# An attention and MLP-mixer block on one core: a unit's first P V products are held back one block where the copy of the preceding unit's sums is far off

## The chip, the cores and the metric

The kernel runs on one core of one Trainium2 chip. The metric is the device time of the whole kernel in microseconds (us); it is one launch.

## What is computed

The reference normalizes `x` (2048 rows of 512 values), scales and shifts it with values made from `c`, and adds attention with 32 heads of 16 values; then it normalizes again and adds a mixer and an MLP. The part that matters here is the attention:

```
q, k, v = qkv[0], qkv[1], qkv[2]                      # 32 heads, 2048 rows, 16 values
scores = einsum("bhqd,bhkd->bhqk", q, k) * (Dh ** -0.5)
p = softmax(scores, axis=-1)
o = einsum("bhqk,bhkd->bhqd", p, v)
x = x + ga * (o.reshape(B, S, D) @ wo)
h = layernorm(x) * (1 + cb) + sb
x = x + gb * mixer_and_mlp(h, w1, w2, w3, w4)
```

## The kernel before

**Stages.** The first 139 us make the first parts of Q, K and V. Attention runs from 139 to 1531 us; its first quarter still has Q, K, V and weight work mixed in as filler, its last 80 us the first rows of the tail. From 1531 us on come the output projection, the mixer and the MLP.

**Units and steps.** Attention has 64 units: four groups of 512 queries times 16 pairs of heads. A unit has 16 key tiles of 128 keys, one step `s` for each, and each step has two halves `j`, one for each head of the pair. For a half, TensorE makes the scores (`sc`, L1009: 128 keys by 512 queries), and beside it, in other rows of the array, the scores of a half 24 steps later in the other orientation (`mb`, L993), of which only the row maximum is wanted. VectorE reduces each `mb` to maxima (`mx`, L989). ScalarE makes the exponential of each `sc` as a 32-bit whole number (`pt`, L1005). The upper and the lower 16 bits of `pt` are used as two f16 operands. The lower ones need a conversion, once for each step over both halves: on GpSimd (L1058), or on ScalarE (the planner's helper, L153) when the planner thinks GpSimd is more than 200 ns further behind than ScalarE (`p_low`).

**P V.** TensorE multiplies `pt` with V into one accumulator `pv` in PSUM. A part with the upper bits of one step is four small matmuls side by side (L1083, called V below); a part with the lower bits of two steps is four more (L1080, called L). A unit has 16 V and 8 L, in the order V V L. There is one accumulator bank for all units: after a unit's last L, ScalarE copies it out (`ac`, L1100, in `ac_copy`), and only then the next unit's first V may write it. Later TensorE sums the copy's rows (`ot`, L1110, eight matmuls in the trace), ScalarE copies that (`sm`, L1117), VectorE takes reciprocals (`rc`, L1125) and GpSimd scales (`osb`, L1121).

**Buffers.** Seven PSUM banks serve `sc` and `mb` in turn (`NSM = 7`; `ot` takes one too), the eighth is the accumulator. There are six `pt` buffers, so the exponential of step s writes where step s-6 was, and has to wait for that step's V and L.

**The order.** The program is written out by hand-made planning in Python at build time: a planner (`Sched`) keeps an estimated time for TensorE (`T["P"]`), ScalarE, VectorE and GpSimd, with fixed costs in ns, and each engine then executes its queue strictly in the order written. Attention is written in blocks. A block is first the *rows*, three halves with their six matmuls (`sc` and `mb`), and then the *column*, all P V parts that are at least two blocks old, one to three of them. A unit has 32 halves and a block 3, so the pattern of blocks against units repeats every 32 blocks, which are three units. At the top of a block stands the accumulator's copy if a unit ended in the block ahead of it; it joins ScalarE's queue ahead of the block's own exponentials. `v_free` is the planner's time at which that copy is done. In the kernel before, the column's loop (L1615) takes parts in order, and stops only ahead of a unit's first V if other parts are already in the same column.

Of the kernel before, what the change touches and what calls it, by code (L numbers as in the profile page):

```python
# [21 lines left out]
P = 128  # L22
KT = D // P
NKT = S // P
# [47 lines left out]
LNPC = 1  # L72
W0G = 1
WSPL = 1
NLOW = 1
CLOW = 1150
OUTW = 7000.0
# [250 lines left out]
def kernel(ctx, tc, A_x, A_wqkv, A_wo, B_w1, B_w2, B_w3, B_w4, c, w_mod, out):  # L328
# [58 lines left out]
    for j in range(2):  # L387
        x = [ident[:, 64 * j + VD * a:64 * j + VD * a + DH + 1] for a in range(3)]
# [29 lines left out]
    sch = Sched()  # L418
# [74 lines left out]
    def load_wm(j):  # L493
# [6 lines left out]
        w = w_mod[:, j * D:(j + 1) * D].rearrange("(k p) n -> p k n", p=P)  # L500
        n = KT // (WSPL if j < 2 else 1)
        for k in range(0, KT, n):
# [395 lines left out]
    def drain(flag):  # L898
        while flag not in done:
            sch.step()  # L900
# [70 lines left out]
    e_exp, e_hi, e_low, v_free, acs = {}, {}, {}, [0.0], []  # L971
# [39 lines left out]
    def row_pair(s, j):  # L1011

        parts = []
        if 0 <= s < NS:
            parts.append((j, score_part(s, j)))
        if s + LEAD < NS:
            parts.append((1 - j, max_part(s + LEAD, 1 - j)))
        parts = [x for _, x in sorted(parts, key=lambda x: x[0])]

        def mms():  # L1020
            for _, mm, _ in parts:
                mm()
        e = sch.put("P", CROW, max(x[0] for x in parts), mms)
        return [partial(x[2], e) for x in parts]
# [20 lines left out]
    def p_low(s):  # L1045

        p = pt[s].rearrange("p j n -> p (j n)")
        o, i = p.bitcast(F16)[:, 0::2], p.bitcast(U16)[:, 0::2]
        ready = e_exp.pop(s) + XX
        g, a = [max(sch.T[e], ready) for e in "GA"]  # L1050
        if g > a + LACT:

            for h in range(NLOW):
                n = 2 * CH // NLOW
                c = slice(h * n, (h + 1) * n)
                e_low[s] = XP["A"] + sch.crit("A", CLOW, ready, partial(act.activation, o[:, c], i[:, c], AF.Copy, scale=0.5))
        else:
            e_low[s] = XP["G"] + sch.crit("G", 1345, ready, lambda: pool.tensor_scalar(  # L1058
                o, i, 0.5, 1.0, op0=OP.mult, op1=OP.mult))

    def pv_ready(s, lo):

        return max(e_low[s], e_low[s + 1]) if lo else max(e_hi.pop(s), v_free[0] if s % NKT == 0 else 0.0)

    def pv_part(s, lo):


        u, kt = divmod(s, NKT)
        if kt == 0 and not lo:
            pv[u] = ap_.tile([P, CH], F32, name="pv", tag="v", bufs=1)  # L1070
        v, acc = vst[u], pv[u]

        def mms():
            for j in range(2):
                for i in range(2):
                    r = 64 * j + 32 * i
                    if lo:
                        c = 128 + 32 * j + (0 if i else 8)
                        n = min(32, 192 - c)
                        te.matmul(acc[r:r + n, :], v[:, kt + i, c:c + n].bitcast(F16), pt[s + i].bitcast(F16)[:, j, 0::2],  # L1080
                                  start=False, stop=kt == NKT - 2, skip_group_check=True)
                    else:
                        te.matmul(acc[r:r + 32, :], v[:, kt, r:r + 32], pt[s].bitcast(F16)[:, j, 1::2],  # L1083
                                  start=kt == 0, stop=False, skip_group_check=True)
        e = sch.put("P", CCOL, 0.0, mms)
        if lo:
            for i in range(2):
                pt.pop(s + i)
                e_low.pop(s + i)
            if kt == NKT - 2:  # L1090
                acs.append((u, e + COUT))

    def ac_copy():
        u, e = acs.pop()
        while u and ("ot", u - 1) not in done:
            sch.step()
        ac = at.tile([P, CH], F32, name="ac", tag="ac", bufs=1)
        vst.pop(u)
        acc = pv.pop(u)
        e = sch.crit("A", cA(), e + PX, lambda: act.activation(ac, acc, AF.Copy))  # L1100
        v_free[0] = e + XP["A"]
        sch.add(o_fin(u, ac, e + XP["A"]), 0)
# [168 lines left out]
    def tail_loads():  # L1271
        rings["0"] = Ring(FRONT, [], "r")
        for _ in range(BR):
            rings["0"].add([("wr", BR)])
            yield sch.wait(T0W)
        for t in range(TPC):
            x1t[t] = fa.tile([P, D], F32, name="x1", tag="x1", bufs=X1F)
            act.dma_start(x1t[t], x_d[t * P:(t + 1) * P])
# [298 lines left out]
    def before(s):  # L1577

        nu, r = divmod(s + 32, 16)
        if r == 0 and 0 < nu < NU:  # L1580
            ci, pr = units[nu]
            drain(("kq", pr // 4))
            if ci:
                drain(("q", pr // 8))
            load_unit(nu)
        nu, r = divmod(s + 6, 16)
        if r == 0 and 0 <= nu < NU:
            drain(("v", units[nu][1] // 8))
            load_v(nu)
        if s == -12:  # L1590
            unit_tiles(at, 2, dve, pool)
# [4 lines left out]
    pvs = [x for s in range(0, NS, 2) for x in ((s, 0), (s + 1, 0), (s, 1))]  # L1596
    due = 0.0
    for k, blk in enumerate(blocks + [[]] * (LAG + CPER)):
        if blk and blk[0] <= LENDS <= blk[-1]:
            sch.most = MOST  # L1600
        for x in blk:
            if x % 2 == 0:
                if x == blk[0]:
                    before(x // 2)
                if x >= 0 and x % 32 == 0:
                    drain(("shift", x // 32))
        if acs:
            ac_copy()
        row = [divmod(x, 2) for x in blk if x < 2 * NS]
        s0 = row[0][0] if row else 0  # L1610
        col = []
        if k >= LAG and (k % CPER == 0 or not blk):

            x = (blocks[min(k - LAG, len(blocks) - 1)] or [-1])[-1]
            while pvs and 2 * (pvs[0][0] + pvs[0][1]) < x and not (col and pvs[0][0] % NKT == 0 and not pvs[0][1]):  # L1615
                col.append(pvs.pop(0))
        t, start = CIN, 0.0
        need = sum((s >= 0) + (s + LEAD < NS) for s, _ in row)
        sch.flush(need)
        banks = sorted(sm.t)  # L1620
        n = 0
        for s, i in row:
            n += (s >= 0) + (s + LEAD < NS)

            start = max(start, banks[n - 1 + 2 * (s < 0)] - t)
            t += CROW
        t += CMID
        for s, i in col:
            start = max(start, pv_ready(s, i) - t)
            t += CCOL  # L1630
        sch.gap(start)
        sch.flush(need)
        sch.T["P"] = max(sch.T["P"], start) + CIN
        low = sorted(e_exp)
        for s, i in row:
            for fn in row_pair(s, i):
                fn()
        for x in blk[1:]:
            if x % 2 == 0:
                before(x // 2)  # L1640
        for s in low:
            p_low(s)
        sch.T["P"] += CMID
        for s, i in col:
            pv_part(s, i)
        sch.T["P"] += COUT
        for e in "ADG":
            sch.misc(e, max(sch.T["P"], sch.T[e]) + TOLE[e])
        if s0 < 0:
            sch.fill(LEADB / 2 * len(blk))  # L1650
        elif sch.gens:
            late = s0 >= NS - T0S
            due += RATE3 if late else RATE if s0 < NS // NC else RATE2
            if due >= (BURST3 if late else BURST if s0 < NS // NC else BURST2):
                sch.fill(due)
                due = 0.0
        if 2 * (NS // NC) - 1 in blk:
            for key in (("v", 1), ("kq", 3), ("q", 0), ("q", 1), "pieces"):
                drain(key)
            qpx.close()  # L1660
            sch.gapmin = GAPMIN2
            ot = o0x.enter_context(tc.tile_pool(name="ot", bufs=1, side="right"))
            for ci in range(1, NC):
                oh[ci] = ot
                osb[ci] = ot.tile([P, TPC, D], F32, name=f"osb{ci}", tag=f"osb{ci}", bufs=1)
            fa = o0x.enter_context(tc.tile_pool(name="fa", bufs=1, side="right"))
            big = {"A4": fa.tile([P, 4 * KT * 2 * P], F32R, name="A")}
            big["A"] = big["A4"]
        if blk and blk[0] <= 2 * (NS - T0L) <= blk[-1]:
            sch.add(tail_loads())  # L1670
        if blk and blk[0] <= 2 * (NS - T0S) <= blk[-1]:
            sch.add(tail(0))
# [54 lines left out]
```

## Time and profile before

| | us |
|---|---|
| median of 3 runs | 2030.32 (2027.38 to 2033.31) |
| the profiled execution | 2025.04 |
| its span, first to last instruction | 2023.3 |
| busy: TensorE, VectorE, GpSimd, ScalarE | 1936.2, 1658.3, 1568.8, 1511.5 |
| granted TensorE clock, mean | 0.990 |

The profiled execution is 5.3 us below the median and has 1.7 us outside its span. In the profile's rows PE is TensorE, PEld its weight loads, DVE VectorE, ACT ScalarE, POOL GpSimd. A row of the timeline has the start, the length, the engine, the line and operation, how many instructions were merged, and in brackets the idle time ahead of the first and what ended it. The matmuls of a merged row overlap each other, so a busy TensorE is not one at its peak.

### The profile page before, as it was taken

How to read it: one execution, taken by the hardware profiler on the slowest of the kernel's cores; microseconds unless marked ns; L12 is line 12 of the kernel's file. 1: busy time of each engine (PE TensorE's matmuls, PEld its weight loads, DVE VectorE, ACT ScalarE, POOL GpSimd, SP SyncE). 2: the span in 40 equal slices, each digit the busy share in tenths (PEclk: the TensorE clock that was granted, in tenths of full speed). 3: DMA queues.
4: the chain of work that ended last, by engine and by line, in shares of the span. 5: the costliest groups of instructions: out<-in, count | busy, mean ns of one | idle time of the engine just before them, and what ended most of it. 6: DMA issues, size and time to landing. Idle time of an engine off the chain costs nothing. (4 is left out here: it accounts for less than half of the span.)

```text
span 2023.3 us, 41663 instructions
## 1 busy us (share of the span) xinstructions
PE 1936.2 (96%) x14456; PEld 1166.2 (58%) x14456; DVE 1658.3 (82%) x2979; ACT 1511.5 (75%) x3085; POOL 1568.8 (78%) x1488
## 2 busy tenths in 40 slices
PE   8999999999999999999999999999998889999999
PEld 5755545454444444444444444444447778888998
DVE  6398788879999999999999999999965786656443
ACT  6438887768999999999999999989984554434443
POOL 6349988879999999999999999999994554425222
PEclk9989999999999999999999999999999999999999
DMA  8877666545353435353434343454414676653541
GB/s 303 234 202 184 156 187 165 133 129 124 72 107 72 107 72 107 72 107 72 101 78 92 87 93 86 93 157 100 90 38 146 233 271 262 233 184 124 189 165 68
DMA packets 185508, 278.01 MB, mean 137 GB/s; under 512 B 117104, under 2 KB 127856, under 8 KB 169008
## 3 DMA queue, kind: packets, MB, share of 16 engines
q1 hardware_dynamic: 181792, 267.20, 49.0%
q10 hardware_dynamic: 2304, 4.20, 0.6%
q0 software_dynamic: 1200, 3.93, 0.5%
q8 instruction: 115, 1.88, 0.4%
q14 instruction: 97, 0.79, 0.1%
HBM read 211.81 MB, written 62.91 MB: 136 GB/s over the span
## 5 line engine op out<-in xcount | busy, mean ns | idle before, releaser
L989 DVE TENSOR_REDUCE mx<-mb 128x1 f32<-128x512 f32 x2048 | 1250.2, 684 | 71.8 <-PE mb L993 62.7
L1058 POOL TENSOR_SCALAR pt<-pt 128x1024 f16<-128x1024 uint16 x953 | 1247.9, 1366 | 77.9 <-ACT pt L1005 74.7
L1005 ACT ACTIVATE pt<-sc 128x512 int32<-128x512 f32 x2048 | 1061.1, 615 | 122.8 <-PE mb L993 97.2
L993 PE MATMUL mb<-kst,qtl 62*128 62x512 f32 x2048 | 780.9, 461 | 21.4 <-ACT pt L1005 9.9
L1009 PE MATMUL sc<-qtl,kst 64*128 64x512 f32 x2048 | 738.7, 448 | 4.2 <-DVE mx L989 1.8
L993 PEld LDWEIGHTS mb<-kst,qtl 62*128 62x128 f32 x2048 | 359.1, 193 | 234.0 <-ACT pt L1005 160.2
L1009 PEld LDWEIGHTS sc<-qtl,kst 64*128 64x128 f32 x2048 | 335.9, 185 | 184.0 <-DVE mx L989 115.5
L1083 PE MATMUL pv<-pt,vst 128*32 128x512 f16 x4096 | 384.6, 397 | 20.6 <-ACT ac L1100 20.6
L1456 POOL TENSOR_TENSOR g<-sq,g 128x256 fp32r<-128x256 f32 (+1 forms) x124 | 98.0, 794 | 184.5 <-ACT g L1455 174.7
L1080 PE MATMUL pv<-pt,vst 128*32 128x512 f16 (+1 forms) x2048 | 221.0, 389 | 2.5 <-POOL pt L1058 2.4
L1083 PEld LDWEIGHTS <-vst 128*32 128x32 bf16 x4096 | 91.7, 93 | 226.6 <-issue 208.1
L358 PE MATMUL w<-A,wr 128*128 128x256 f32 (+1 forms) x520 | 155.6, 300 | 0.1
L356 PE MATMUL w<-A,wr 128*128 128x256 f32 (+1 forms) x520 | 155.4, 300 | 0.2 <-ACT A L350 0.2
L360 PE MATMUL w<-A,wr 128*128 128x256 f32 (+1 forms) x520 | 155.0, 299 | 0.0
L1452 ACT ACTIVATE sq<-w 128x256 f32<-128x256 f32 (+1 forms) x130 | 52.1, 402 | 123.2 <-PE w L360 113.9
L356 PE MATMUL w<-wr,g 128*128 128x512 f32 x270 | 106.7, 395 | 2.4 <-DMA wr<-Ws 2.4
L360 PE MATMUL w<-wr,g 128*128 128x512 f32 x270 | 106.2, 393 | 0.2 <-POOL g L1456 0.2
L358 PE MATMUL w<-wr,g 128*128 128x512 f32 x270 | 106.2, 393 | 0.0
L1434 DVE SCALAR_TENSOR_TENSOR sq<-sq,w 128x256 f32<-128x256 f32 (+1 forms) x130 | 58.1, 449 | 54.2 <-ACT sq L1454 53.8
L356 PEld LDWEIGHTS w<-A,wr 128*128 128x128 f32 x520 | 100.8, 194 | 1.5 <-ACT A L350 0.5
L358 PEld LDWEIGHTS w<-A,wr 128*128 128x128 f32 x520 | 100.9, 194 | 1.2 <-DVE A L346 0.4
L360 PEld LDWEIGHTS w<-A,wr 128*128 128x128 f32 x520 | 100.8, 194 | 0.5 <-issue 0.5
(156 smaller groups left out, 2124.9 us busy)
## 6 DMA issues: line engine op xcount, KB each, us to landing
wr<-Ws SPq DMA_DIRECT2D x66, 1024.0 KB, 5.9
vst<-Vs SPq DMA_DIRECT2D x64, 768.0 KB, 5.7
kst<-Ks SPq DMA_DIRECT2D x126, 384.0 KB, 6.3
Ws<-wr SPq DMA_DIRECT2D x14, 1024.0 KB, 6.3
qtl<-Qs SPq DMA_DIRECT2D x128, 96.0 KB, 4.4
Vs<-vt SPq DMA_DIRECT2D x32, 384.0 KB, 4.4
Ks<-qk SPq DMA_DIRECT2D x16, 512.0 KB, 4.0
Qs<-qk SPq DMA_DIRECT2D x16, 512.0 KB, 3.0
```

Source lines behind the costliest of these rows:

```text
L356: te.matmul(o, lh, rh, start=first, stop=False)
L358: te.matmul(o, lh, rl, start=False, stop=False)
L360: te.matmul(o, ll, rh, start=False, stop=last)
L989: end = sch.crit("D", 605, e + PX, lambda: dve.reduce_max(mxs[u][:, j, g, c:c + 1], b, axis=AX.X))
L993: return ready, lambda: te.matmul(b, lhs, kst[u % 3][r, c * CH:(c + 1) * CH], start=True, stop=True), after
L1005: ea = sch.crit("A", 480, e + PX, lambda: act.activation(pt[s][:, j], b, AF.Exp))
L1009: return ready, lambda: te.matmul(b, kst[u % 3][r, kt * P:(kt + 1) * P], qst[u][r], start=True, stop=True), after
L1058: e_low[s] = XP["G"] + sch.crit("G", 1345, ready, lambda: pool.tensor_scalar(o, i, 0.5, 1.0, op0=OP.mult, op1=OP.mult))
L1080: te.matmul(acc[r:r + n, :], v[:, kt + i, c:c + n].bitcast(F16), pt[s + i].bitcast(F16)[:, j, 0::2], start=False, stop=kt == NKT - 2, skip ...
L1083: te.matmul(acc[r:r + 32, :], v[:, kt, r:r + 32], pt[s].bitcast(F16)[:, j, 1::2], start=kt == 0, stop=False, skip_group_check=True)
L1434: dve.scalar_tensor_tensor(sq, sq, 1.0, b, op0=OP.add, op1=OP.mult)
L1456: ("G", cG(n), lambda: pool.tensor_tensor(lo, sq, hi, op=OP.subtract)), (None, 0, end), bank=b)
```

## The change

A constant `VLATE = 1500.0` is added. Ahead of a unit's first V the column now also stops where it is still empty, if the block has rows and the planner expects the accumulator's copy to be done more than 1500 ns after TensorE's present time:

```diff
+VLATE = 1500.0
...
-            while pvs and 2 * (pvs[0][0] + pvs[0][1]) < x and not (col and pvs[0][0] % NKT == 0 and not pvs[0][1]):
+            while pvs and 2 * (pvs[0][0] + pvs[0][1]) < x:
+                if pvs[0][0] % NKT == 0 and not pvs[0][1] and (col or row and v_free[0] > sch.T["P"] + VLATE):
+                    break
                 col.append(pvs.pop(0))
```

The parts come in a fixed order, so such a block has rows alone, and the next block's column has the parts of both. This happens at 20 of the 63 unit starts, counted from 0: units 1, 4, 5, 7 and 15, and then every third from 19 to 61. Since the planner's times differ from there on, other instructions move too. In the rows below line numbers of the changed kernel are one higher than before (L1084 is V, L1081 is L, L994 `mb`, L1010 `sc`, L1101 the copy, L1111 `ot`, L154 the conversion on ScalarE).

**TensorE, end of unit 54, the block in which the copy is late.** Before:

```order
L993 MATMUL mb<-kst_1105,qtl_1103 128x512
L1009 MATMUL sc<-qtl_965,kst_967 128x512 x2
L993 MATMUL mb<-kst_1105,qtl_1103 128x512 x2
L1009 MATMUL sc<-qtl_965,kst_967 128x512
L1083 LDWEIGHTS vst
L1083 MATMUL pv<-pt,vst 32x512
```

and in the changed kernel:

```order
L994 MATMUL mb<-kst_1105,qtl_1103 128x512
L1010 MATMUL sc<-qtl_965,kst_967 128x512 x2
L994 MATMUL mb<-kst_1105,qtl_1103 128x512 x2
L1010 MATMUL sc<-qtl_965,kst_967 128x512 x2
L994 MATMUL mb<-kst_1105,qtl_1103 128x512 x2
L1010 MATMUL sc<-qtl_965,kst_967 128x512 x2
L994 MATMUL mb<-kst_1105,qtl_1103 128x512
L1084 LDWEIGHTS vst
L1084 MATMUL pv<-pt,vst 32x512
```

Before, six score matmuls are followed by V V L, six more, and V. Now twelve score matmuls stand together, and V V L V behind them.

**TensorE, where the copy of unit 54 is summed (`ot`).** Before:

```order
L1083 MATMUL pv<-pt,vst 32x512
L1110 MATMUL ot<-smat,ac 128x34 x4
L993 MATMUL mb<-kst_1105,qtl_1103 128x512
L1009 MATMUL sc<-qtl_965,kst_967 128x512 x2
L993 MATMUL mb<-kst_1105,qtl_1103 128x512 x2
L1009 MATMUL sc<-qtl_965,kst_967 128x512
```

and now:

```order
L1084 MATMUL pv<-pt,vst 32x512
L1111 MATMUL ot<-smat,ac 128x34 x4
L1010 MATMUL sc<-qtl_965,kst_967 128x512
L994 MATMUL mb<-kst_1105,qtl_1103 128x512 x2
L1010 MATMUL sc<-qtl_965,kst_967 128x512 x2
L994 MATMUL mb<-kst_1105,qtl_1103 128x512
```

`ot` stood ahead of the rows of the second block after the late copy (they begin with `mb`); now it stands one block later (rows that begin with `sc`).

**ScalarE, end of unit 15, where nothing is held back.** Before:

```order
L1005 ACTIVATE pt<-sc 128x512 x21
L153 ACTIVATE pt<-pt 128x1024
L1100 ACTIVATE ac<-pv 128x512
L1005 ACTIVATE pt<-sc 128x512 x6
L1117 ACTIVATE sm<-ot 128x136
```

and now:

```order
L154 ACTIVATE pt<-pt 128x1024
L1006 ACTIVATE pt<-sc 128x512 x12
L1101 ACTIVATE ac<-pv 128x512
L1006 ACTIVATE pt<-sc 128x512 x6
L1118 ACTIVATE sm<-ot 128x136
```

The conversion stood right ahead of the copy; now twelve exponentials lie between them. The copy of unit 12 has lost its conversion in the same way. In all, ScalarE has 76 conversions instead of 71 and GpSimd 948 instead of 953; every other kind of instruction has the same count as before.

## The prediction

> **What bounds the kernel now.** I read the busy time by stage first. The columns are PE, PEld, DVE, ACT and POOL busy us (with counts), then the granted clock and the DMA share:
>
> ```profile
> 139.30:480.00 340.70, 331.84 (x2575) 178.10 (x2575) 284.69 (x485) 272.72 (x565) 304.91 (x261) 1.00 0.62 162
> 480.00:1458.00 978.00, 947.14 (x8064) 448.96 (x8064) 938.55 (x1632) 904.22 (x1792) 938.25 (x801) 1.00 0.44 93
> 1531.00:2023.30 492.30, 463.54 (x2715) 415.67 (x2713) 298.34 (x595) 213.60 (x489) 199.34 (x287) 0.98 0.51 188
> ```
>
> The change acts in the first two rows. In the long one, 978 us, three engines are equally full: TensorE 96.8%, VectorE and GpSimd 96.0%. None has much idle time to give, and VectorE's 39 us (978 - 938.55) and GpSimd's 40 us bound what any reordering there can bring. In the first row TensorE alone is full (97.4%). Next the list of waits, of the whole run:
>
> ```profile
> PE pv L1083 <- ACT ac L1100: 20.6, 19, 1.2
> ```
>
> The columns are us in total, times and the longest. And the groups by line, VectorE's maxima within 480 to 1458 us (busy, mean ns, idle ahead and what ended it):
>
> ```profile
> L989 DVE TENSOR_REDUCE mx<-mb 128x1 f32<-128x512 f32 x1536 | 934.0, 684 | 33.1 <-PE mb L993 26.1 <-PE sc L1009 3.6
> ```
>
> TensorE waits 20.6 us in all for the accumulator's copy, at 19 of 63 unit starts. That is the wait which the change is about, and about 1.1 us each time. The second row says what it can be worth: VectorE's idle time ahead of maxima, 33.1 us. So I need to see how much of that idle time comes from the late copy. One of the 17 regular places (the ends of units 12, 15 and so on to 60), unit 57, TensorE first, in order of time:
>
> ```profile
> 1396.33 0.51 PE L993 MATMUL mb<-kst,qtl 62*128 62x512 f32 x1
> ...
> 1397.99 0.64 PE L1083 MATMUL pv<-pt,vst 128*32 128x512 f16 x8 [1.16 <-ACT ac L1100]
> 1398.44 0.41 PE L1080 MATMUL pv<-pt,vst 128*32 128x512 f16 x4
> 1398.78 0.50 PE L1009 MATMUL sc<-qtl,kst 64*128 64x512 f32 x1
> ...
> 1399.46 0.50 PE L993 MATMUL mb<-kst,qtl 62*128 62x512 f32 x1
> 1399.89 0.41 PE L1083 MATMUL pv<-pt,vst 128*32 128x512 f16 x4
> 1400.23 1.08 PE L1110 MATMUL ot<-smat,ac 128*128 128x34 f32 x8
> 1401.24 0.50 PE L993 MATMUL mb<-kst,qtl 62*128 62x512 f32 x1
> ...
> 1401.82 0.39 PE L993 MATMUL mb<-kst,qtl 62*128 62x512 f32 x1
> 1402.15 0.41 PE L1083 MATMUL pv<-pt,vst 128*32 128x512 f16 x4
> ...
> 1402.94 0.49 PE L1009 MATMUL sc<-qtl,kst 64*128 64x512 f32 x1
> ```
>
> I call the block whose V V L starts at 1397.99 block A, and the next ones B (rows at 1398.78), C (rows at 1401.24) and D (rows at 1402.94). ScalarE, VectorE and GpSimd at that place:
>
> ```profile
> 1394.70 1.58 ACT L1005 ACTIVATE pt<-sc 128x512 int32<-128x512 f32 x3 [0.39 <-PE mb L993]
> 1396.14 1.35 ACT L153 ACTIVATE pt<-pt 128x1024 f16<-128x1024 uint16 x1
> 1397.35 0.59 ACT L1100 ACTIVATE ac<-pv 128x512 f32<-128x512 f32 x1
> 1397.81 3.14 ACT L1005 ACTIVATE pt<-sc 128x512 int32<-128x512 f32 x6
> 1401.35 0.28 ACT L1117 ACTIVATE sm<-ot 128x136 f32<-128x136 f32 x1 [0.40 <-PE ot L1110]
> 1401.81 2.31 ACT L1005 ACTIVATE pt<-sc 128x512 int32<-128x512 f32 x4 [0.18 <-PE mb L993]
> ```
>
> ```profile
> 1396.75 1.88 DVE L989 TENSOR_REDUCE mx<-mb 128x1 f32<-128x512 f32 x3
> 1399.35 1.89 DVE L989 TENSOR_REDUCE mx<-mb 128x1 f32<-128x512 f32 x3 [0.72 <-PE mb L993]
> 1401.78 1.89 DVE L989 TENSOR_REDUCE mx<-mb 128x1 f32<-128x512 f32 x3 [0.55 <-PE mb L993]
> 1403.58 0.19 DVE L1125 RECIPROCAL rc<-sm 128x8 f32<-128x8 f32 x1
> 1403.77 0.19 DVE L1039 TENSOR_REDUCE mf<-mx 128x8 f32<-128x32 f32 x1
> 1403.87 19.94 DVE L989 TENSOR_REDUCE mx<-mb 128x1 f32<-128x512 f32 x33
> ...
> 1439.08 0.69 DVE L989 TENSOR_REDUCE mx<-mb 128x1 f32<-128x512 f32 x1 [0.20 <-PE mb L993]
> ...
> 1448.70 10.86 DVE L989 TENSOR_REDUCE mx<-mb 128x1 f32<-128x512 f32 x18 [0.39 <-PE mb L993]
> ```
>
> ```profile
> 1398.58 6.64 POOL L1058 TENSOR_SCALAR pt<-pt 128x1024 f16<-128x1024 uint16 x5 [0.88 <-ACT pt L1005]
> ```
>
> The copy is late because a conversion (1.35) stands ahead of it on ScalarE. VectorE then idles 0.72 + 0.55 = 1.27 us: first because block B's rows stand behind V V L, then because `ot` stands ahead of block C's rows. From 1403.87 it runs almost without a gap; the only other gaps of the three units, until 1458.3, that the rows mark are 0.20 and 0.39. So VectorE sets the pace there, and **the measure of the change is when VectorE starts block D's maxima, 1403.87 now.**
>
> **The change at that place, worked out.** It removes V V L from between the rows of A and B. The work is the same, so I move it by the gaps between starts in the rows above. ScalarE's order up to the exponentials of A and B is unchanged.
>
> First, when can B's rows run? There are seven banks, and A's rows hold six. B's six matmuls take the one that is left, then those which A's work gives back, in the planned order: the last pair takes those of A's third maximum and second exponential. VectorE's maxima come every 0.60 us (33 in 19.94), A's last three starting about 1396.75, 1397.35 and 1397.94. ScalarE's second exponential of A stands alone in a narrower stretch of the same view:
>
> ```profile
> 1398.29 0.63 ACT L1005 ACTIVATE pt<-sc 128x512 int32<-128x512 f32 x1
> ```
>
> It follows the first by 0.48 (from 1397.81) and ends at 1398.92. A freed bank's matmul starts about 0.05 later: A's own last pair at 1396.33 came 0.05 after the exponentials of 1394.70 + 1.58 = 1396.28. So B's last pair starts at 1398.97. **TensorE's wait for the copy has become a wait for banks.**
>
> Then TensorE goes on without a wait. Rows to the first V: 0.33 (1401.82 to 1402.15), so V V L V starts at 1399.30; the copy has been done since 1397.94. Three parts to the next rows take 0.79 (1402.15 to 1402.94), and one part more half of the 0.45 from the first V of A to its L (1397.99 to 1398.44): 1.02 for four. C's rows start at 1400.32, its V L V 0.91 later (1401.24 to 1402.15) at 1401.23, `ot` after 0.79 at 1402.02, and D's rows after another 1.01 (1400.23 to 1401.24) at **1403.03, against 1402.94 now**.
>
> VectorE: A's maxima end its use at 1398.54, and B's follow without a gap, since their inputs are there (the last at 1398.97 + 0.54 = 1399.51, before 1399.73): the 0.72 is gone. It is free at 1400.33. But C's first maximum must wait for 1400.32 + 0.54 = 1400.86 (0.54: 1401.24 to 1401.78), an idle 0.53. It is free at 1402.66, does the small reduction (0.19), and waits for D's rows until 1403.57, an idle 0.72, with the reciprocal of 0.19 still to do: 1403.76 in equal terms, against 1403.87. **The idle 1.27 becomes 0.53 + 0.72 = 1.25; the gain is 0.1 us** at each of 15 places: 1.5 us.
>
> GpSimd's 0.88 stays, since it waits for A's exponentials, whose place on ScalarE does not change. What the other moves hide behind: `sm` and the reciprocal come a block later, and nobody waits for them. With `ot` and the planner's times the DMA issues on SP move by single places; they load units that start many blocks later, so I cost them at nothing (DMA share 0.44); if that cover went, one late load would cost a part of a block's 1.7 us (1401.24 to 1402.94).
>
> [...]
>
> **The other places.** At units 12 and 15 the copy loses the conversion ahead of it. VectorE now, after unit 12's end:
>
> ```profile
> 481.80 1.89 DVE L989 TENSOR_REDUCE mx<-mb 128x1 f32<-128x512 f32 x3 [0.73 <-PE mb L993]
> 484.23 0.69 DVE L989 TENSOR_REDUCE mx<-mb 128x1 f32<-128x512 f32 x1 [0.55 <-PE mb L993]
> ```
>
> At an ordinary `ot` the idle is 0.20 (the row at 1439.08), so up to 1.28 - 0.20 = 1.08 is saved at each; at least 0, if the conversion delays something at its new place. I take half for both: 1.1 us. The five conversions more on ScalarE cost 5 x 1.35 = 6.8 us of an engine that has 74 us free in the long stage, and save GpSimd as many; nothing on the path.
>
> Before 480 us five unit starts are held back, of which one waits now:
>
> ```profile
> 245.17 0.63 PE L1083 MATMUL pv<-pt,vst 128*32 128x512 f16 x8 [0.50 <-ACT ac L1100]
> ```
>
> TensorE is the bound there, so this is 0.5 us if the held-back block finds banks. The four others wait for nothing that is removed: between nothing and a wait for banks of 1.16 each, in place of filler that now covers the copy. VectorE is only 84% busy there (284.69 of 340.70) and so gives banks back early; I take 0.
>
> Sum: 1.5 + 1.1 + 0.5 = 3.1 us off. Against the profiled execution: 2025.04 - 3.1 = 2021.9; that execution is 5.3 below the median, so the median becomes 2030.3 - 3.1 = **2027.2 us**. After 1531 us the work stays the same and the end moves with attention's.
>
> **The rivals.**
>
> *The wait is really removed.* B's rows come early, and VectorE keeps the 0.72: if TensorE has slack hidden in the overlapping matmuls, D's rows come by 1402.4 and the gap before them doesn't grow. For it: TensorE is shown busy through many waits of its weight loads. Against it: the steps that I moved are measured from start to start and have that slack in them. It would give 15 x 0.72 = 10.8 and 1.6 as above: 12.4 off, 2017.9.
>
> *The held-back parts pile up (slower).* Four parts, `ot` and their followers stand behind a last pair that waits for a bank; and since there are six `pt` buffers, B's third exponential needs the buffer that the L of V V L V frees. By my count that L ends at 1399.30 + 0.45 + 0.40 = 1400.15, and ScalarE, at its step of 0.48, is there five exponentials after 1397.81, at 1400.21: no margin. ScalarE's gaps after it (0.40 and 0.18) cover 0.58. It decides from where TensorE reaches D's rows 0.5 us later than I count: VectorE would then lose 0.4 at each of 15 places, 6 us, and if the four early places without a wait lose half of 1.16, 2.3 more; with 1.1 back from units 12 and 15: 7.2 slower, 2037.5.
>
> *It does not do what it says.* The 1500 compares planner's times; four of 20 places have no wait now, and two waits go by accident. If the planned times are off at the new places too, the gain is only the accident, 0 to 2.2 us: 2029, hardly to be told from the forecast.
>
> **How the numbers follow.** The forecast with its last rival has 0.48, the removed wait 0.29, the pile-up 0.20, and 0.03 is for what I have not seen. What a measurement of this kernel can tell is about 0.3%, 6.1 us: below 2024.2 is faster, above 2036.4 slower. The forecast's own range is 2023 to 2031 (0 to 2.2 from units 12 and 15, up to 1.5 more or less from the regular places, and a median's scatter of some 3 us). Faster takes the removed wait and a little of the forecast's edge, 0.31; slower takes most of the pile-up, 0.20; the same 0.49. The range for 8 in 10 reaches to the removed wait's time and nearly to the pile-up's: 2017 to 2037.
>
> **What would show it.** Right: the wait of V for `ac` nearly gone from the list; at each regular place the last pair of B's rows waiting for ScalarE's exponentials; VectorE with two gaps of about 0.5 and 0.7 ahead of C and D instead of ahead of B and C; three units still taking 60.9 us; no gap at units 12 and 15. Wrong: three units in 60.2 us or less (the wait was removed), or in 61.3 or more (the pile-up), or ScalarE waiting for an L ahead of B's third exponential.

## The result, and the profile after

| | before | changed |
|---|---|---|
| median, same chip, 17 runs each | 2030.67 (2023.53 to 2035.81) | 2036.10 (2031.78 to 2040.67) |
| the profiled execution | 2025.04 | 2040.67 |
| its span | 2023.3 | 2038.9 |
| granted TensorE clock in it | 0.990 | 0.983 |

The ratio is 1.0029, with an interval of 1.0019 to 1.0039: the change costs 5.4 us by the medians, 3.9 to 7.9 by the interval. One execution of the experiments below, at 2078.5 us, was in a slower state of the chip and is left out of its ratio. The profiled execution of the changed kernel is the slowest of its 17, that of before is faster than all but one of its own 17. The two traces therefore differ by 15.6 us, most of it scatter, and I compare stretches of them, not their ends. The largest part, 7.1 us, lies behind the last copy (499.8 us against 492.7). Over all the traces of this document that stage takes 491.7 to 500.5 us, and 498.8 in one that holds nothing back, so it cannot be laid on the change.

The stages first, in the columns of the prediction's rows (busy us with counts, then clock, DMA share, GB/s), changed kernel:

```profile
480.00:1458.00 978.00, 956.13 (x7970) 450.17 (x7966) 928.45 (x1615) 895.72 (x1776) 923.91 (x789) 0.99 0.44 92
1531.00:2038.90 507.90, 476.40 (x2800) 425.54 (x2797) 302.81 (x603) 220.25 (x500) 208.17 (x298) 0.97 0.51 187
```

In the same 978 us VectorE does 1615 instructions instead of 1632 and is busy 10 us less, TensorE does 94 matmuls fewer and is busy 9 us *more*. The clock column has gone from 1.00 to 0.99 in the first row, from 0.98 to 0.97 in the last. TensorE's waits of the whole run (total us, times, longest):

```profile
PE mb L994 <- ACT pt L1006: 17.0, 36, 0.5
...
PE mb L994 <- DMA kst<-Ks: 2.0, 1, 2.0
...
PE pv L1084 <- ACT ac L1101: 1.8, 2, 1.5
```

The wait for the copy has gone from 20.6 us at 19 places to 1.8 at 2. In its place the score matmuls wait for ScalarE to free banks, 36 times instead of 22, 17.0 us instead of 9.9. So the edit did what it says. VectorE got nothing of it, its idle time ahead of maxima rather grew (before, then changed):

```profile
L989 DVE TENSOR_REDUCE mx<-mb 128x1 f32<-128x512 f32 x2048 | 1250.2, 684 | 71.8 <-PE mb L993 62.7
L990 DVE TENSOR_REDUCE mx<-mb 128x1 f32<-128x512 f32 x2048 | 1248.7, 679 | 75.1 <-PE mb L994 60.6
```

**A place where it went as forecast.** The end of unit 24 in the changed kernel, TensorE in order of time, with the bank wait in brackets, and VectorE at the same place:

```profile
727.48 0.50 PE L994 MATMUL mb<-kst,qtl 62*128 62x512 f32 x1 [0.50 <-ACT pt L1006]
727.48 0.74 PE L1010 MATMUL sc<-qtl,kst 64*128 64x512 f32 x2
727.97 0.50 PE L994 MATMUL mb<-kst,qtl 62*128 62x512 f32 x1
728.39 0.64 PE L1084 MATMUL pv<-pt,vst 128*32 128x512 f16 x8
```

```profile
722.76 6.66 DVE L990 TENSOR_REDUCE mx<-mb 128x1 f32<-128x512 f32 x11
729.97 1.89 DVE L990 TENSOR_REDUCE mx<-mb 128x1 f32<-128x512 f32 x3 [0.56 <-PE mb L994]
731.96 0.18 DVE L1040 TENSOR_REDUCE mf<-mx 128x8 f32<-128x32 f32 x1
732.76 0.20 DVE L1126 RECIPROCAL rc<-sm 128x8 f32<-128x8 f32 x1 [0.62 <-ACT mf L1041]
```

VectorE goes through the maxima of A and B without a gap (11 in one row), then idles 0.56 ahead of C and 0.62 ahead of D. What ends the second gap is the reciprocal, which waits for ScalarE and stands ahead of D's maxima in VectorE's order; these start at 732.88, 0.12 us after it has started.

**A place where it did not.** Unit 30's end, the same views:

```profile
849.51 0.60 PE L994 MATMUL mb<-kst,qtl 62*128 62x512 f32 x1 [0.50 <-ACT pt L1006]
849.51 1.02 PE L1010 MATMUL sc<-qtl,kst 64*128 64x512 f32 x2
850.00 0.79 PE L994 MATMUL mb<-kst,qtl 62*128 62x512 f32 x1
850.72 1.05 PE L1084 MATMUL pv<-pt,vst 128*32 128x512 f16 x8
```

```profile
845.38 6.14 DVE L990 TENSOR_REDUCE mx<-mb 128x1 f32<-128x512 f32 x10
853.36 1.89 DVE L990 TENSOR_REDUCE mx<-mb 128x1 f32<-128x512 f32 x3 [1.85 <-PE sc L1010]
```

The order and the bank wait (0.50) are the same, but the matmuls behind the wait are longer (eight V 1.05 us instead of 0.64, `mb` 0.79 instead of 0.50), and VectorE idles 1.85 us instead of 0.56. Rows by windows of the clock's own step show why, unit 24's end first and then unit 30's:

```profile
723.47:726.88 3.41, 3.24 (x22) 1.42 (x18) 3.41 (x6) 3.19 (x6) 3.23 (x3) 1.00 1.01 163
726.88:730.29 3.41, 2.91 (x27) 1.40 (x26) 2.85 (x6) 3.37 (x8) 2.71 (x3) 1.00 0.68 214
...
846.42:849.83 3.41, 2.76 (x17) 1.27 (x13) 3.41 (x7) 3.41 (x7) 2.67 (x3) 0.99 0.97 150
849.83:853.24 3.41, 3.41 (x24) 1.45 (x24) 1.69 (x3) 2.18 (x5) 3.41 (x3) 0.51 0.47 177
```

In the last window TensorE's clock is halved (0.51). The trace's clock records hold such stretches of 3.41 us, at times two or three in a row, and within a trace all begin on one grid of 3.41 us (the 15 of this trace to within 4 ns). At these two places, where the thin time around the bank wait falls into one window of the grid (17 matmuls in the one from 846.42 on), the next window runs at half clock; where the grid cuts it in two (22 and 27), none does. So the same block is hit or spared by the accident of where the grid lies.

The other places bear this out. Four traces (this one and, from the experiments below, that of the regular places alone and two with a weight load moved) have 60 held-back regular places, and 17 of them have half clock behind the copy. At 16 of the 17 the copy starts 1.49 to 2.23 us after a line of the grid, and no spared place has its copy in that range (the seventeenth, unit 60 of this trace, is hit at 0.66). What the change made thin can be counted too. Of all stretches of 3.41 us around a regular place, the thinnest has 8 matmuls starting in it (`ot` aside) in the changed kernel and 16 in the kernel before, though TensorE's wait is shorter now (0.50 us instead of 1.16): the late V V L stood there. Before has 12 at the ends of units 24, 36 and 48, and its half clock at regular places, three times in four traces, came at 36, 24 and 24.

Price and number of these stretches, three units each (copy to copy), the changed kernel first and then before. The clock is the first of the last three columns:

```profile
726.34:787.31 60.97, 59.73 (x505) 28.34 (x504) 58.65 (x104) 56.35 (x113) 58.69 (x51) 1.00 0.44 89
848.37:910.57 62.20, 60.98 (x505) 28.86 (x504) 58.73 (x104) 56.35 (x114) 58.91 (x51) 0.97 0.42 88
```

```profile
968.22:1030.33 62.11, 60.08 (x504) 28.79 (x504) 58.84 (x103) 56.60 (x113) 59.04 (x51) 0.97 0.42 88
1397.35:1458.27 60.92, 59.02 (x504) 27.94 (x504) 58.77 (x104) 56.51 (x114) 58.64 (x51) 1.00 0.43 89
```

A half-clock stretch costs 1.2 us here, in either kernel (62.20 against 60.97, 62.11 against 60.92). In this trace six of the fifteen regular places of the changed kernel have one, in that of before one of seventeen. By the runs: over 83 executions of the kernel before on three chips, the time rises by 0.66 us for each us of span times (1 - mean clock), with a correlation of 0.83; the mean of that quantity is 24.0 us there and 32.1 in the 17 runs of the changed kernel. 8.0 x 0.66 = 5.3 us (32.07 less 24.04 before rounding): as much as the change costs. That is a correlation, and an execution that waits longer for another reason could show a lower clock too (in the tail of before, 6.8 us of half clock go with each of two waits of 5.6 us); the experiments test it.

**A second place.** Between the copies of units 54 and 57 the changed trace loses 4.8 us more (66.95 against 62.17). Some 1.2 of this is the half-clock stretch behind unit 54's own copy, one of the six above. For the rest, TensorE waits 2.0 us for unit 58's K (0.75 before), and a half-clock stretch of 6.8 us follows. SyncE's queue shows what moved, before and then changed:

```profile
1349.24 0.59 SPq L132 DMA_DIRECT2D wr<-Ws  x1
1349.93 0.37 SPq L132 DMA_DIRECT2D qtl<-Qs  x1
1350.35 0.42 SPq L132 DMA_DIRECT2D kst<-Ks  x1
1350.87 0.49 SPq L132 DMA_DIRECT2D qtl<-Qs  x1
1351.40 0.51 SPq L132 DMA_DIRECT2D kst<-Ks  x1
1351.95 0.44 SPq L132 DMA_DIRECT2D wr<-Ws  x1
```

```profile
1353.44 0.59 SPq L133 DMA_DIRECT2D wr<-Ws  x1
1355.11 0.32 SPq L133 DMA_DIRECT2D qtl<-Qs  x1
1355.48 0.42 SPq L133 DMA_DIRECT2D kst<-Ks  x1
1356.17 0.30 SPq L133 DMA_DIRECT2D qtl<-Qs  x1
1358.55 0.30 SPq L133 DMA_DIRECT2D kst<-Ks  x1
```

Before, the second of the three loads of tail weights (`wr`) stands ahead of unit 58's Q and K and the third behind them; now it is the third that stands ahead. The second K load was issued 2.2 us after that `wr` (1351.40 after 1349.24), now 5.1 us after (1358.55 after 1353.44). For 2.1 us of these SyncE's queue stands still ahead of the K load, a wait that the trace puts down to a transfer of `wr`; before, it has no such wait there.

So there were two suspects, the clock at the held-back blocks and the late K load, and a rival: that holding back costs by itself, through banks or the order of the work.

### The profile page after: what moved, and what is told of

It reads as the page before. It is cut to its first block, busy times and chain, and to the rows that moved or that the text cites. A ratio compares the mean times of both kernels' runs of the same rounds, so it can differ in the third digit from the quotient of the medians.

```text
span 2038.9 us, 41656 instructions
## 1 busy us (share of the span) xinstructions
PE 1959.4 (96%) x14456; PEld 1174.9 (58%) x14456; DVE 1660.9 (81%) x2979; ACT 1515.3 (74%) x3090; POOL 1564.0 (77%) x1483
## 5 line engine op out<-in xcount | busy, mean ns | idle before, releaser
L994 PE MATMUL mb<-kst,qtl 62*128 62x512 f32 x2048 | 789.8, 464 | 28.2 <-ACT pt L1006 17.0
L1010 PE MATMUL sc<-qtl,kst 64*128 64x512 f32 x2048 | 741.3, 450 | 4.6 <-DVE mx L990 3.2
L994 PEld LDWEIGHTS mb<-kst,qtl 62*128 62x128 f32 x2048 | 361.6, 194 | 257.8 <-ACT pt L1006 178.8
L1010 PEld LDWEIGHTS sc<-qtl,kst 64*128 64x128 f32 x2048 | 337.7, 186 | 173.6 <-DVE mx L990 102.0
L1084 PE MATMUL pv<-pt,vst 128*32 128x512 f16 x4096 | 389.3, 401 | 1.8 <-ACT ac L1101 1.8
L1081 PE MATMUL pv<-pt,vst 128*32 128x512 f16 (+1 forms) x2048 | 225.7, 393 | 1.8 <-POOL pt L1059 1.4
L1084 PEld LDWEIGHTS <-vst 128*32 128x32 bf16 x4096 | 91.1, 94 | 211.1 <-issue 191.4
L154 ACT ACTIVATE pt<-pt 128x1024 f16<-128x1024 uint16 x76 | 105.3, 1385 | 0.0
L359 PEld LDWEIGHTS w<-A,wr 128*128 128x128 f32 x520 | 102.0, 196 | 1.3 <-DVE A L347 0.5
L357 PEld LDWEIGHTS w<-A,wr 128*128 128x128 f32 x520 | 101.6, 196 | 1.0 <-ACT A L351 0.2
```

What stands on the lines that cost most here:

```text
L357: te.matmul(o, lh, rh, start=first, stop=False)
L359: te.matmul(o, lh, rl, start=False, stop=False)
L994: return ready, lambda: te.matmul(b, lhs, kst[u % 3][r, c * CH:(c + 1) * CH], start=True, stop=True), after
L1010: return ready, lambda: te.matmul(b, kst[u % 3][r, kt * P:(kt + 1) * P], qst[u][r], start=True, stop=True), after
```

## The experiments

Each ratio is to the kernel before on the same chip, with its 95% interval.

**One part of the change alone.** The stop at a unit's first V only from unit 19 on (15 places), or only before (5 places):

```diff
-                if pvs[0][0] % NKT == 0 and not pvs[0][1] and (col or row and v_free[0] > sch.T["P"] + VLATE):
+                if pvs[0][0] % NKT == 0 and not pvs[0][1] and (col or row and pvs[0][0] >= 300 and v_free[0] > sch.T["P"] + VLATE):
```

(and `< 300` for the other).

> V is held back only at the 15 regular places (units 19, 22 and so on to 61); units 1, 4, 5, 7 and 15 are as before. Two theories. Clock: a held-back block leaves TensorE with less to do in one window of 3.4 us, after which its clock is granted at half for 3.4 us; seven of the 15 places show that in the changed kernel's trace, and three units then take 62.1 to 62.4 us instead of 60.95. It expects 5 to 8 such dips within 602 to 1475 us and 2036 to 2039 us (1.2 x 5 to 7 above before's 2030.7). Plan: the loss comes from the new plan of the first units and of the last 80 us of attention, the dips come and go by themselves: 2029 to 2032 us, dips as few as before (one).

> V is held back only at units 1, 4, 5, 7 and 15; from unit 19 on nothing is held back, the copies are waited for as before. Clock: no dip is added at the regular places, so 2029 to 2032 us. Plan: the loss stays, 2034 to 2037 us.

The regular places alone: 1.0029 [1.0017, 1.0040], the whole loss again, at a mean clock of 0.984 against 0.988, and in its trace five half-clock stretches just behind a regular copy. (The expectation's seven of 15 in the changed kernel's trace are six; the seventh in that stretch is the one behind the wait for K.) The early places alone: 1.0052 [1.0034, 1.0070], worse than the whole change. Its 2040.5 us lie above the ranges of both theories. Its trace shows half clock at two regular places that hold nothing back, units 30 (3.4 us) and 57 (6.8 us), and the largest loss in one place:

```profile
PE mb L994 <- DMA kst<-Ks: 5.5, 1, 5.5
```

Here two `wr` loads were issued straight ahead of unit 58's Q and K, 10.2 us at half clock go with the wait, and the three units to 57 take 70.95 us instead of 62.17. That is 8.8 of the 18.6 us by which this trace is behind; 6.9 more lie behind the last copy. So the two halves lose in different ways, and their losses do not add up.

**The clock without the hold-back's waits touched.** The changed kernel, with the score matmuls of the held-back blocks issued twice into the same banks, same values; the second round fills TensorE's thin time:

```diff
-            for _, mm, _ in parts:
-                mm()
+            for _ in range(1 + twice):
+                for _, mm, _ in parts:
+                    mm()
...
-            for fn in row_pair(s, i):
+            for fn in row_pair(s, i, twice=row and not col and s0 >= 0 and bool(pvs)):
```

> The changed kernel, but in a block whose V is held back each of the six score matmuls is issued twice into the same bank (same result; 120 matmuls more, and those of the very first blocks), so that TensorE is busier in the window in which it otherwise waits. Clock: the dips at held-back blocks are gone or down to one or two, three units take 60.9 to 61.2 us, and the time falls by 3 to 7 us against the changed kernel, to 2029 to 2033 us, though there is more work. Plan, or a theory that banks or the later parts cost the time: no gain, 2036 us or a little more (up to 20 x 0.6 us).

1.0013 [1.0005, 1.0022] at a mean clock of 0.989: more than half of the loss is gone although TensorE has more to do, and no regular place has a half-clock stretch. The late K load is still in the trace (1.7 us).

**No conversion ahead of the copy.** The kernel before, but a conversion that the planner would put on ScalarE ahead of a copy is decided anew behind it:

```diff
+    lows = []
...
-        if g > a + LACT:
+        if g > a + LACT and ends:
+            e_exp[s] = ready - XX
+            lows.append(s)
+        elif g > a + LACT:
...
+        while lows:
+            p_low(lows.pop())
```

> The kernel before, with nothing held back, but a conversion that the planner would give to ScalarE in the block in which a unit ends is decided again after the copy, so that no conversion stands ahead of a copy. If the late copy costs what VectorE idles there (1.27 less the usual 0.2), 17 places give up to 18 us: 2013 to 2026. If its work only comes back elsewhere, as the held-back V's did, 2028 to 2032. Clock theory: no dips within 602 to 1475 us.

1.0050 [1.0037, 1.0063], at before's mean clock (0.989). Nothing of the hoped gain came. From 480 to 1458 us, TensorE's wait for the copy and then VectorE's maxima:

```profile
PE pv L1087 <- ACT ac L1104: 2.7, 8, 0.5
```

```profile
L990 DVE TENSOR_REDUCE mx<-mb 128x1 f32<-128x512 f32 x1514 | 921.0, 684 | 47.5 <-PE mb L994 37.8 <-PE sc L1010 8.8
```

The wait for the copy is down to 2.7 us from 18.6 in that stretch, yet VectorE's idle time ahead of maxima rises from 33.1 to 47.5. A late copy taken away is not time won: the regular pattern with the late copy was good for VectorE, and the order that replaces it is worse. Of the 14.0 us by which this trace is behind, 5.1 lie between the copies of units 18 and 54, without a half-clock stretch among them, so an order can cost at full clock too. Another 6.8 lie between units 54 and 57, with a wait of 1.3 us for K and two half-clock stretches of 6.8 us; how these divide is not settled.

**The K load.** The changed kernel with the third `wr` load held until unit 58's tiles are there:

```diff
-        for _ in range(BR):
+        for i in range(BR):
+            if i == 2:
+                yield lambda: 58 in qst
```

and two edits of the kernel before: the order on SyncE as the change made it (`yield sch.wait(T0W if i else 0.0)` in place of `yield sch.wait(T0W)`), and both later `wr` loads behind K (`if i: yield lambda: 57 + i in qst`).

> The changed kernel, with the third of the three 1 MB loads of tail weights issued behind the K loads of unit 58, as it stood before; in the changed kernel it stands ahead of them. Theory that this load costs: TensorE's wait for K near 1365 us goes from 2.04 back to 0.8 or less, the clock is not granted at half after it, units 54 to 57 take 62 to 63.5 us instead of 66.95, and the time is 2 to 4 us below the changed kernel's: 2032 to 2034. Theory that the regular places are all: within 1 us of the changed kernel, 2035 to 2037.

> The changed kernel with the third tail-weight load behind unit 58's K loads, as in e5, measured a second time. Theory (the late K load costs part of the loss): 1.001 to 1.002, and the three units to 57 take 62.5 us or less instead of 67. Rival (what the wait for K costs is made up later, or given back to clock dips): 1.003 again, with the wait gone from the trace.

> The kernel before, with nothing held back; only the second and third 1 MB loads of tail weights are issued earlier, so that SP's queue has the order of the changed kernel there (third load ahead of the K loads of unit 58). Theory of the load: the wait for K goes from 0.75 to about 2, a dip of the clock follows, units 54 to 57 take 65 to 67 us instead of 62.2, and the time is 2 to 4 us above before's: 2032 to 2034. Otherwise: within 1 us of before.

> The kernel before, with the second and third 1 MB loads of tail weights issued behind the K loads of units 58 and 59. Theory of the load: the wait of 0.75 for K near 1362 us goes, units 54 to 57 take 61 to 61.5 instead of 62.2, 1 us less in all: 2028 to 2030. If the weights then come late for the tail, its first projection waits and the time rises.

The kernel before with the other order: 1.0036 [1.0020, 1.0052], and the wait in its trace is 3.0 us. With both later loads behind K: 1.0006 [0.9994, 1.0018], no gain to be had there. But in the changed kernel, the load behind K gives 1.0028 [1.0015, 1.0041], and a second time 1.0028 [1.0014, 1.0042]: no better than the 1.0029 without it, though in both traces the place is mended (62.4 and 63.7 us for the three units instead of 66.95, and no wait for K; one of 1.0 to 1.1 us, put down to ScalarE, stands in its place). Both traces are among the shortest executions of their runs (2031.3 and 2028.5 us, where the medians are 2033.9 and 2035.2) and have half clock at three regular places, so they show less of the loss than the usual execution. The order of the loads can cost 7 us by itself; that it is a part of this change's loss is not shown.

**Both together.** First for the regular places alone (hold-back from unit 19 on, scores twice there, load behind K), then for the whole change:

> V held back at the 15 regular places alone, score matmuls of such blocks issued twice, and the third weight load behind the K loads. If the clock's dips at held-back blocks and that load are the whole loss of the regular places, this is the same as before: 2028 to 2031 us, three units 60.9 to 61.2. If holding back costs something else as well, 2032 or more. If the plan of the last 80 us matters, the stage from the last copy on stays 3 to 5 us longer than before's 492.7.

> The changed kernel with both repairs: in the held-back blocks the score matmuls are issued twice, into the same banks (the same values), and the third tail-weight load is issued behind unit 58's K loads. Theory (the clock dips at the held-back blocks and the late K load make up the loss): no half-clock stretch at the ends of units 18 to 60, the three units to 57 within 62.5 us, mean clock about 0.989, ratio to the kernel before 0.999 to 1.002. Rival (the hold-back itself costs, by banks or by the order of the work after it): the ratio stays at about 1.003, with the dips gone.

1.0006 [0.9995, 1.0018] and 1.0003 [0.9994, 1.0013]: the same as before. With the load behind K in both, the matmuls issued twice are all that separates 1.0028 from 1.0003, and the mean clock goes from 0.985 to 0.990. Unit 30's end with both, TensorE and then VectorE:

```profile
850.01 0.51 PE L994 MATMUL mb<-kst,qtl 62*128 62x512 f32 x1 [0.52 <-ACT pt L1006]
...
850.93 0.64 PE L1085 MATMUL pv<-pt,vst 128*32 128x512 f16 x8
```

```profile
844.66 7.26 DVE L990 TENSOR_REDUCE mx<-mb 128x1 f32<-128x512 f32 x12
852.50 1.89 DVE L990 TENSOR_REDUCE mx<-mb 128x1 f32<-128x512 f32 x3 [0.58 <-PE mb L994]
...
855.29 0.20 DVE L1127 RECIPROCAL rc<-sm 128x8 f32<-128x8 f32 x1 [0.61 <-ACT mf L1042]
```

The bank wait is still there (0.52), and so are VectorE's two gaps (0.58 and 0.61). Only the half clock behind the wait is gone (eight V take 0.64 again), and the loss with it. It is not a matter of where the grid happened to lie: in the four traces with the matmuls issued twice, ten held-back copies start 1.49 to 2.23 us after a line of the grid, where all 16 were hit without, and none is hit. The thinnest 3.41 us at a regular place has at least 14 matmuls starting there, not 8. What holding back costs by itself can be no more than the interval leaves, 0.13% or 2.6 us; a small cost is not excluded, as the mean clock is a little above that of before (0.990 against 0.988). One expectation failed: the three units to 57 took 63.5 us instead of 62.5 or less, with a half-clock stretch behind a wait of 1.3 us put down to ScalarE.

**The long waits of the tail.** If TensorE's thin windows cost that much, the tail's long ones should cost more (waits of 5.6, 5.6 and 3.1 us, with 6.8, 6.8 and 3.4 us of half clock at them). The kernel before, with redundant transposes of a tile that is there ahead of three that wait for a normalized tile; and the same on top of the changed kernel with both repairs:

```diff
+                    if fill and i == nt - 1:
+                        for _ in range(fill):
+                            te.transpose(b3[:, j, i * P:(i + 1) * P], src(k, 0), ident)
+                        fill = 0
                     te.transpose(b3[:, j, i * P:(i + 1) * P], src(k, i), ident)
```

> The kernel before, with redundant transposes (40, 40 and 24, of a tile that is there, into a place that the awaited transposes then overwrite) ahead of three transposes of the tail which wait 5.6, 5.6 and 3.1 us for a normalized tile. The work that counts is unchanged. Theory (a long wait of TensorE sets off the half clock behind it): the half-clock stretches at about 1575, 1637 and 1712 us (6.8, 6.8 and 3.4 us) are gone, the tail after 1531 us runs at a clock of 0.99 or more instead of 0.98, and the whole is 3 to 8 us faster, 0.996 to 0.9985. Rival (the redundant transposes delay what waits behind them, or the tail is bound by VectorE there): 1.000 or above.

> The changed kernel with the rows twice, the third weight load behind unit 58's K loads, and the redundant transposes in the tail. If the parts add up: f1's ratio and f3's together, 0.996 to 1.000.

The stretch around the two waits of 5.6 us, before and then with the transposes:

```profile
1560.00:1600.00 40.00, 30.26 (x182) 27.16 (x181) 32.19 (x69) 22.43 (x48) 24.23 (x39) 0.91 0.53 184
1630.00:1650.00 20.00, 14.38 (x67) 12.76 (x67) 17.45 (x33) 11.97 (x23) 12.83 (x15) 0.83 0.75 273
```

```profile
1560.00:1600.00 40.00, 32.61 (x223) 29.15 (x222) 32.63 (x70) 22.20 (x48) 24.76 (x40) 1.00 0.50 179
1630.00:1650.00 20.00, 18.74 (x115) 16.99 (x114) 18.38 (x34) 12.33 (x24) 13.44 (x15) 1.00 0.74 277
```

The half clock is gone from both, and the mean clock of all runs rises from 0.988 to 0.992. The time is 0.9992 [0.9981, 1.0003]: 1.6 us less by the ratio, not told from nothing, where 3 to 8 were expected. On top of the repaired change it is 1.0000 [0.9991, 1.0009]. So half clock behind the tail's waits costs little (1.6 us in all by the ratio, or nothing), and behind the held-back blocks of attention much (1.2 us a stretch). No version here is shown to beat the kernel before.

**The mean clock is no price by itself.** By the 0.66 of the correlation, the transposes, which bring span times (1 - mean clock) from 24.2 down to 15.7 us, should have won 5.6 us, and the last version, with 14.2, 6.6; measured were 1.6 and nothing. And in the profiled execution of the kernel before with both later `wr` loads behind K (2033.56 us, its median 2030.05) the clock stands at 0.95 through nearly the whole span, yet attention runs as before. Nine units of before, then the same stretch of that execution:

```profile
785.00:968.00 183.00, 177.26 (x1512) 83.98 (x1512) 176.02 (x307) 169.75 (x337) 175.95 (x151) 1.00 0.43 89
785.00:968.00 183.00, 177.26 (x1514) 84.00 (x1514) 175.97 (x307) 169.81 (x336) 175.99 (x151) 0.95 0.43 89
```

So what costs here is half clock just where VectorE comes to wait for TensorE (1.85 us instead of 0.56 at unit 30's end), and that 8.0 x 0.66 met the loss so closely is in part luck. What shows the cause is the pair of versions that differ in the matmuls issued twice alone, and the places that the grid hits in one and not in the other.

## Why the prediction was wrong

The forecast was 2027.2 us, 3.1 less than before; the change costs 5.4. The time of 2036.1 lies within the range, at its upper end, but the sign was wrong. That the range holds it is luck: its upper end was set by the pile-up, which did not come about as it was counted.

- **The wait turns into a wait for banks: right.** The forecast had B's last pair waiting for ScalarE's exponential; the trace has 0.50 us there. VectorE's gaps were forecast as 0.53 and 0.72 and are 0.56 and 0.62. Three units were to take 60.9 us still; they take 60.97 where the clock holds. The gain of 0.1 us at a place is not there, though: from the copy's start to block D's maxima it was 6.52 us at unit 57 before and 6.41 by the forecast, and it is 6.53 to 6.56 at seven of the nine spared places (at the two others `ot` comes later still). With the repairs, too, that part is worth nothing that can be measured. And VectorE does wait for the later `sm`: its second gap ends at the reciprocal, where the prediction had nobody wait.
- **The step that failed: moving the work "by the gaps between starts in the rows above".** It gave the term of 15 x 0.1 = 1.5 us for the regular places, and it takes each matmul's duration as given. The change made TensorE's wait shorter, but it took V V L out of the place, so that the thinnest 3.41 us has 8 matmuls starting instead of 12 to 16, and the clock fell to half in the window behind at three to six of fifteen places in the traces, against one of seventeen. The row of the tail that the prediction quoted with a clock of 0.98 showed that the clock does fall in this kernel; no term and no rival asked what the change does to it. What it measured: no gain at the spared places and a loss of 1.2 us at each that is hit; issuing the matmuls twice takes the ratio from 1.0028 to 1.0003, some 5 us.
- **Units 12 and 15, 1.1 us gained: wrong.** Their late copies are gone as forecast, but the changed kernel is 2.39 us ahead when unit 12's copy starts and 0.02 when unit 18's does. The three units from 12 took 61.85 us instead of 60.85, the next three 62.89 instead of 61.52, at full clock. The experiment without conversions ahead of the copy shows the same: the late copy's gap is not simply saved.
- **The early places, 0.5 us: too small, and of no use.** Most of the 2.39 us at unit 12 seems to come from there (1.5 us in the trace with the early places alone, 0.2 with the regular ones alone); it is what is lost again by unit 18. (Only four of the prediction's five starts lie before 480 us; unit 15's lies at 519.)
- **"The DMA issues on SP move by single places ... I cost them at nothing": mis-sized in the trace.** One load passed the Q and K loads of unit 58, and where the prediction named a part of a block's 1.7 us as the price, the three units lost 4.8 us there, some 1.2 of it by unit 54's own half-clock stretch. Whether the median has any of it stays open, as the load's repair alone changed nothing.
- **The end "moves with attention's": nearly.** With both repairs the stage after the last copy takes 494.9 us instead of 492.7; 16 filler matmuls moved from attention to behind it, and TensorE waits 20.9 us for `xn` in the whole run instead of 19.6. The changed kernel's trace has 499.8 us, within the scatter of the traces.
- **The rivals.** The wait was not really removed: no three units in 60.2 us. The pile-up had the right sign and nearly the right time (2037.5), but the time by luck: what it foresees is not at the spared places, where no exponential waits for a `pt` buffer. At five of the six places with half clock an exponential does wait for one, 0.69 to 0.88 us (put down to GpSimd's conversion four times, to an L once). So a pile-up comes only where the clock has fallen, and that the rival did not have. The change does what it says.

## What to carry to other kernels

When work is moved around a wait on TensorE, look not only at whether the wait is hidden but at how TensorE's thin time is spread (here 8 matmuls starting in the thinnest 3.41 us instead of 12 to 16), and read the clock column by window: a busy share of 96%, the same in both traces, did not show what halved clocks did. The shorter wait (0.50 us instead of 1.16) was worth nothing here, since VectorE started block D's maxima no earlier (6.53 to 6.56 us after the copy's start at seven of the nine spared places, 6.52 at unit 57 before); so follow the engine that sets the pace through to the end of the pattern. And when the order of issues changes, look for the one large load that has passed a smaller one that is needed soon (here a `wr` load of 1024 KB ahead of K loads of 384 KB: TensorE's wait for K went from 0.75 to 2.0 us).

## What the hardware showed that was not expected

- At six regular places of the changed kernel's trace the clock was halved for 3.41 us behind windows in which no single wait was longer than 0.50 us. The same block, with the same wait, was hit or spared by where it lay on the grid of 3.41 us (hit, but for one place, with the copy 1.49 to 2.23 us after a line of it), so the number of places hit differs between traces, three to six of fifteen in four of them; the 17 runs of the changed kernel lie between 2031.8 and 2040.7 us.
- Redundant matmuls, six more in each held-back block, made the kernel faster: from 1.0028 to 1.0003 with the load behind K. The number of matmuls that start in a window went with the half clock where idle time did not: with 8 at the thinnest and 0.50 us idle six of fifteen places were hit in the changed kernel's trace, with 16 and 1.16 us idle none in that of before. In the tail, 104 redundant transposes raised the clock nearly as much (0.988 to 0.992 against 0.985 to 0.990), and the 0.0008 that came of it cannot be told from nothing. Why half clock costs so little there was not tried; the work behind those waits may be set by another engine.
- A recorded clock of 0.95 through nearly a whole execution left attention's pace as it was (the same 307 VectorE instructions in 183 us), where half clock for 3.41 us at a held-back block cost 1.2 us.
- On one queue, unit 58's K loads stand behind one `wr` load or another. With the second of three ahead TensorE waited 0.75 us for K, in one trace not at all; with the third instead 1.3 to 3.0; with both 5.5; with none ahead it did not wait for K. In four of the five traces with the third ahead the queue stood still 2.1 to 3.8 us for a transfer of `wr` before it issued K; why the third holds it and the second does not was not tried.
